# Attention and two MoE layers in one kernel: each engine's own register and branch in a weight change, low-part products last, attention's logits unjoined, and the order at the front and the border

## The chip, the cores and the metric

The kernel runs on one core of a Trainium2 chip. The metric is the device time of one execution in microseconds (us). A core has five engines with a queue of their own each, which run side by side and wait for one another through semaphores: PE (TensorE, the matmuls; its weight loads are listed as PEld), DVE (VectorE), ACT (ScalarE), POOL (GpSimd) and SP (SyncE, which here only starts transfers). An engine works through its queue strictly in order, so an instruction that waits holds up whatever stands behind it.

## The reference

The inputs are float32. Attention has 4 batches, 8 heads, 768 positions and 64 columns a head; a query sees 8 global and 96 local keys. Its output, as 3072 rows of 512, goes through a top-1 mixture of 8 experts with 1024 hidden units, and the result through a second one, whose logits also get a bias by modality.

```python
scores = scale * np.matmul(q, k.transpose(0, 1, 3, 2)) + bias   # masked: global or local keys
a = softmax(scores); attn = np.matmul(a, v)
x = attn.transpose(0, 2, 1, 3).reshape(3072, 512)
# MoE, twice with weights of its own
logits = x @ w_gate                  # second time: + modality_bias[modality_id]
expert_idx = np.argmax(logits, axis=1)
gate_w = softmax(logits)[arange(N), expert_idx]
for e in range(8):
    out[mask] = gate_w[mask, None] * (np.maximum(x[mask] @ w1[e], 0.0) @ w2[e])
```

## The kernel before

Every float32 operand of a product is split in a high part (float16) and a low part (bfloat16), and a product of two such operands is three matmuls: high by high, high by low, low by high.

**What sets the order.** `Timeline.at(t, fn)` gives each step a time that is a plain number, and `run` emits the steps sorted by it. The numbers come from the tables `OFF`, `MOFF`, `NEXTM`, `LASTM`, `LAST0` and `SOFF`. They don't make an instruction start at a time; they set in what order the steps stand in the queues of all engines, DMA issues included. The program is made under a manual schedule, so nothing reorders it later.

**Attention** works on 24 units of 128 queries, each with four head pairs. For a unit, PE computes the scores `sp` (L624, 24 products), DVE takes the row maximum `nm` (L636, one a head pair's half), ACT the exponentials `e`; PE transposes them (`et`, L653/654), ACT and DVE split them (`eh` L660, `el` L666), and PE multiplies by the values (`xp`, L681). DVE scales the sums to a row of the attention's output (`rs` L688, `row` L702). That row is then routed for the first MoE: PE transposes it (`xtp`, L712, step "rt"), ACT takes its high part (`rxh`, L717, step "rh"), DVE the low part (`rxl`, L722, step "rl"), PE forms the eight logits of each row (`lp`, L421, step "lg"), and DVE picks the largest: `join` (L428, L429) adds the two column groups of `lp` to `lg`, `MAX` (L437) and `MAX_INDEX` (L441) find the expert, L445 and L451 make a one-hot row `oh`. PE ranks it (`pr`, L472/473), DVE takes the position (`t`, L478), the count `acc` goes on (L482, on POOL in attention), and a scatter of POOL (L490) writes the row to a DRAM buffer `xs`, sorted by expert.

```python
ops = [(0, 2 * E, c) for c in range(4)] + [(1, E, c) for c in range(4)]      # logits, before: wg_hl holds
                                                                           # 8 high and 8 scaled low columns
```

**The MoEs** work on slots of 128 rows of one expert. A slot has four parts p of the hidden units. For each, `mm1` is 24 products (`hp`, L895), ACT and DVE split the result (`hh` L905, `hl` L906), and `mm2` is 6 products of 512 columns (`y`, L914). Weights in use lie in SBUF as h1, l1, h2, l2; if the next slot has another expert, `change` (L921, an `If` on a register read from a table) lets ACT cast the high part (`h`, L124) and DVE subtract the low part (`l`, L352) from float32 weights that were staged before. Such an `If` is in every engine's queue. `refill` (L934) is an `If` of SP, under which SP starts the transfers (`st`, L339) of an expert's weights, and "f00", "f01", "f10", "f11" are its four places in a slot. The first slots, FRONT (two in the first MoE, three in the second), are chosen before the whole table is known. After the fixed slots (27 and 23) a tail runs only if the count asks for it: `If` at L1107, also in every queue. Between the two MoEs the rows of the first are split (`r`, L955/956), stored (`x_d`, L970), loaded back transposed (`x2t`, L975), routed as above with a `join` of three operations (L428, L429, L431), and counted by the products `cp` (L497/498), from which DVE works out the second table. In the slots 17 to 19 of the first MoE SP also loads the rows of the second's three FRONT slots (step "lload": `mx` L847, `mm` L849, under the `If` at L1055).

The lines that the change touches moved in the changed kernel by 5 to 10; the prose uses those of the kernel before.

Of the kernel before, what the change touches and what calls it, by code (L numbers as in the profile page):

```python
# [12 lines left out]
BF16 = mybir.dt.bfloat16  # L13
# [54 lines left out]
NEXTM = {"p": 6.1, "pc": 6.2}  # L68
LAST0 = {
# [35 lines left out]
def kernel(  # L105
# [178 lines left out]
    wg_hl = [const.tile([128, 4, 2 * E], F16, name=f"wghl{m}") for m in range(2)]  # L284
    late = const.tile([32, 2], F32, name="late")
# [19 lines left out]
    def constants():  # L305
        nc.vector.tensor_scalar(out=rowoff_b, in0=rowoff[0:1, :], scalar1=-1.0, scalar2=None, op0=ALU.mult)
        nc.vector.memset(meta[:, :, 0:NM - E], 0.0)
        nc.vector.memset(meta[:, :, 2:3], 1.0)
        nc.vector.tensor_copy(out=meta[:, :, 1], in_=tok_id)
        nc.vector.tensor_copy(out=mod_f[:, 1], in_=mod_i[:, :, 0])  # L310
        nc.vector.tensor_scalar(out=mod_f[:, 0], in0=mod_f[:, 1], scalar1=-1.0, scalar2=1.0, op0=ALU.mult, op1=ALU.add)
        for i in range(2):
            nc.vector.tensor_tensor(out=mod_b[:, i], in0=mod_f[:, i].unsqueeze(2).to_broadcast([128, NU, E]),
                                    in1=bias_sb[:, i].unsqueeze(1).to_broadcast([128, NU, E]), op=ALU.mult)
        nc.vector.tensor_tensor(out=meta[:, :, NM - E:NM], in0=mod_b[:, 0], in1=mod_b[:, 1], op=ALU.add)
        for m in range(2):
            nc.vector.tensor_copy(out=wg_hl[m][:, :, 0:E], in_=wg_sb[m])
            nc.vector.tensor_tensor(out=wg_sb[m], in0=wg_sb[m], in1=wg_hl[m][:, :, 0:E], op=ALU.subtract)
            nc.vector.tensor_scalar(out=wg_hl[m][:, :, E:2 * E], in0=wg_sb[m], scalar1=LOW, scalar2=None, op0=ALU.mult)

        nc.vector.tensor_scalar(out=late[:, 0:1], in0=slot_id, scalar1=float(AHEAD), scalar2=None, op0=ALU.is_equal)
        nc.vector.tensor_scalar(out=late[:, 1:2], in0=slot_id, scalar1=float(AHEAD), scalar2=None, op0=ALU.is_gt)
# [94 lines left out]
    def logits(m, xt):  # L417
        lp = bank("C", "lp")
        ops = [(0, 2 * E, c) for c in range(4)] + [(1, E, c) for c in range(4)]
        for n, (x, w, c) in enumerate(ops):  # L420
            nc.tensor.matmul(out=lp[:, 0:w], lhsT=xt[x][:, c, :], rhs=wg_hl[m][:, c, 0:w],  # L421
                             start=(n == 0), stop=(n == len(ops) - 1), skip_group_check=True)
        return lp

    def join(lp, more=None):

        lg = small.tile([128, E], F32, tag="lg", name="lg")
        nc.vector.tensor_copy(out=lg, in_=lp[:, E:2 * E])  # L428
        nc.vector.scalar_tensor_tensor(out=lg, in0=lg, scalar=1.0 / LOW, in1=lp[:, 0:E], op0=ALU.mult, op1=ALU.add)  # L429
        if more is not None:  # L430
            nc.vector.tensor_tensor(out=lg, in0=lg, in1=more, op=ALU.add)  # L431
        return lg
# [453 lines left out]
    def mm1(m, s, p):  # L886
        d = mst[m][s]
        hp = bank("AD"[p % 2], "hp")[:, 0:256].rearrange("p (j c) -> p j c", j=2)
        for j in range(2):
            fs = slice(j * 128, (j + 1) * 128)  # L890
            n = 0
            for c in range(4):
                for w, x in ((h1, 0), (h1, 1), (l1, 0)):
                    r = d["x"][:, 4 * x + c, :]
                    nc.tensor.matmul(out=hp[:, j, :], lhsT=w[p][:, c, fs], rhs=r.bitcast(BF16) if x else r,  # L895
                                     start=(n == 0), stop=(n == 11))
                    n += 1
# [10 lines left out]
    def mm2(m, s, p):  # L908
# [3 lines left out]
        for j in range(2):  # L912
            for i, (hx, w) in enumerate((("hh", h2), ("hh", l2), ("hl", h2))):
                nc.tensor.matmul(out=d["y"], lhsT=d[hx, p][:, j, :], rhs=w[p][:, j, :],  # L914
                                 start=(p == 0 and j == 0 and i == 0), stop=(p == NP - 1 and j == 1 and i == 2))

    def change(m, s, p, i, step):

        if (m, s) not in regs:
            regs[m, s] = val(m, FCHG, s, [ET.Activation, ET.DVE], 1)  # L920
        with tc.If(regs[m, s] > 0):  # L921
            split(p, i, steps=(step,))
# [136 lines left out]
    def slots(tl, m, t0, t_table):  # L1059
# [21 lines left out]
        for s in range(fixed):  # L1081
# [9 lines left out]
            if m == 0:  # L1091
                offs = (LASTM if last else NEXTM if s == fixed - 2 else {}).items()
# [40 lines left out]
    for u in range(NU):  # L1133
# [3 lines left out]
        for nm, fn in (("tq", lambda u: t_in(u, "q")), ("tk", lambda u: t_in(u, "k")),  # L1137
# [3 lines left out]
                       ("lg", route_l), ("pm", lambda u: pick_m(st[u], join(st[u]["lp"]), st[u]["row"])),  # L1141
# [3 lines left out]
                       ("wa", lambda u: place_a(0, st[u], eng_of("wa"))), ("place", route_p)):  # L1145
# [73 lines left out]
```

## Time and profile before

| | us |
|---|---|
| three runs | 851.1, 852.2 (median), 865.14 |
| the profiled execution | 861.72 |
| its span | 860.2 |
| PE busy in the span | 775.3 (90%) |
| DVE busy | 485.0 (56%) |
| ACT busy | 395.5 (46%) |
| POOL busy | 311.0 (36%) |
| attention alone, with all engines full | 40 to about 200 |
| first MoE's fixed slots | about 228 to 560 |
| second MoE's fixed slots | about 604 to 846 |

Busy time is what an engine spent on instructions of its own, without branches, semaphores and DMA issues. The mean granted clock of TensorE was 0.976 of full speed. The profiled execution is some 9.5 us above the median of the three runs; sums are made against its 861.72.

### The profile page before, as it was taken

To read this page: it belongs to the slowest core of one execution; us is meant where nothing else is said; L and a number is where in the kernel's file an instruction comes from. 1 tells how busy PE (TensorE), PEld (TensorE's weight loads), DVE (VectorE), ACT (ScalarE), POOL (GpSimd) and SP (SyncE) were. 2 spreads that over 40 slices of the span, in tenths; PEclk is the share of its full clock that TensorE was granted. 3 is DMA by queue.
4 is the path that set the end of the run, shared out by engine and by line. 5 is a ranking of instruction groups with operands and counts; after the bars stand their busy time and mean duration, and the time that the engine had idled before them with its cause. 6 is when DMAs were issued, how large, how long until landed. Compare 5 with 4: busy or idle time off the path is not lost. (4 is left out here: it accounts for less than half of the span.)

```text
span 860.2 us, 29737 instructions
## 1 busy us (share of the span) xinstructions
PE 775.3 (90%) x9892; PEld 588.0 (68%) x9892; DVE 485.0 (56%) x1830; ACT 395.5 (46%) x859; POOL 311.0 (36%) x522
## 2 busy tenths in 40 slices
PE   4888988887799999999998898878999999999994
PEld 3777777776566777677766676555777777777773
DVE  4899999999627575757664747454111134111142
ACT  4788888788225253435523425331222244222251
POOL 5579887886532333233323241011111111111110
PEclk9899999998799999999999999999999999999998
DMA  8878676594666988898887877523822228222100
GB/s 138 226 194 235 152 181 157 135 299 127 236 141 181 217 197 248 255 192 238 230 222 174 221 199 185 155 57 72 242 66 53 52 78 219 61 54 56 41 26 18
DMA packets 227581, 133.97 MB, mean 156 GB/s; under 512 B 177148, under 2 KB 199676, under 8 KB 227360
## 3 DMA queue, kind: packets, MB, share of 16 engines
q1 hardware_dynamic: 220896, 112.10, 53.6%
q0 software_dynamic: 6320, 19.37, 6.1%
q8 instruction: 83, 1.36, 0.7%
q14 instruction: 138, 1.13, 0.5%
q10 hardware_dynamic: 144, 0.00, 0.0%
HBM read 79.54 MB, written 33.77 MB: 132 GB/s over the span
## 5 line engine op out<-in xcount | busy, mean ns | idle before, releaser
L895 PE MATMUL hp<-mx,h 128*128 128x128 f16 x3520 | 324.1, 221 | 7.7 <-ACTq L921 3.5
L895 PE MATMUL hp<-mx,l 128*128 128x128 f16 x1760 | 310.6, 221 | 13.7 <-DVE l L352 11.0
L895 PEld LDWEIGHTS <-h 128*128 128x128 f16 x3520 | 277.6, 99 | 46.0 <-issue 5.8
L906 DVE SCALAR_TENSOR_TENSOR hl<-hp,hh 128x256 bf16<-128x256 f32 x220 | 92.9, 423 | 255.2 <-ACT hh L905 131.3
L905 ACT ACTIVATE hh<-hp 128x256 f16<-128x256 f32 x220 | 84.0, 382 | 267.4 <-PE hp L895 234.6
L895 PEld LDWEIGHTS <-l 128*128 128x128 bf16 x1760 | 173.6, 99 | 15.6 <-DVE l L352 12.3
L914 PE MATMUL y<-h,hh 128*128 128x512 f16 x440 | 168.1, 382 | 0.0
L914 PE MATMUL y<-l,hh 128*128 128x512 bf16 x440 | 168.1, 382 | 0.0
L914 PE MATMUL y<-h,hl 128*128 128x512 f16 x440 | 167.6, 381 | 0.0
L352 DVE TENSOR_TENSOR l<-st,h 128x1024 bf16<-128x1024 f32 x84 | 105.4, 1256 | 42.5 <-ACTq L921 16.0
L914 PEld LDWEIGHTS <-hh 128*128 128x128 f16 x880 | 77.5, 98 | 53.8 <-issue 1.5
L124 ACT CAST h<-st 128x1024 f16<-128x1024 f32 x88 | 91.3, 1043 | 43.8 <-SPq L934 21.7
L964 POOL DMA_INDIRECT out_dram<-o,ti x26 | 27.2, 1045 | 227.7 <-ACTq L921 191.4
L490 POOL DMA_INDIRECT xs<-r,posi x29 | 33.4, 1153 | 181.1 <-DVEq L921 63.1
L643 ACT ACTIVATE e<-e,nm 128x232 f32<-128x232 f32 (+1 forms) x192 | 81.7, 471 | 6.2 <-DVE nm L636 5.7
L914 PEld LDWEIGHTS <-hl 128*128 128x128 bf16 x440 | 43.3, 98 | 53.1 <-issue 1.6
L666 DVE TENSOR_TENSOR el<-et,eh 128x512 bf16<-128x512 f32 (+1 forms) x96 | 60.9, 635 | 2.5 <-ACT eh L660 2.5
L636 DVE CUSTOM_DVE_ANT_0 e<-sp,bias_mid 128x232 f32<-128x232 f32 x160 | 58.0, 384 | 1.2 <-PE xp L681 0.8
L660 ACT CAST eh<-et 128x512 f16<-128x512 f32 (+1 forms) x96 | 51.9, 540 | 9.7 <-PE et L654 7.9
L624 PE MATMUL sp<-kt,qt 64*128 64x128 f16 (+3 forms) x1056 | 42.7, 219 | 14.3 <-DVE nm L636 14.1
L654 PE MATMUL et<-ident,e 128*128 128x128 f32 x192 | 48.4, 286 | 4.5 <-ACT e L643 2.2
L653 PE MATMUL et<-ident,e 128*128 128x128 f32 x160 | 43.0, 295 | 5.7 <-DVE el L666 2.8
(211 smaller groups left out, 1082.1 us busy)
## 6 DMA issues: line engine op xcount, KB each, us to landing
st<-in_moe_w_dram SPq DMA_DIRECT2D x88, 512.0 KB
mxf<-xs SPq DMA_DIRECT2D x29, 266.0 KB
x_d<-r SPq DMA_DIRECT2D x29, 256.0 KB
ld_k<-in_k_dram SPq DMA_DIRECT2D x24, 256.0 KB
ld_q<-in_q_dram SPq DMA_DIRECT2D x24, 256.0 KB
ld_v<-in_v_dram SPq DMA_DIRECT2D x24, 256.0 KB
row<-xg SPq DMA_DIRECT2D x24, 256.0 KB
xs<-empty SPq DMA_DIRECT2D x18, 266.0 KB
```

What stands on the lines that cost most here:

```text
L124: nc.scalar.copy(out=out, in_=in_)
L352: (nc.vector if engines[i][1] == "V" else nc.gpsimd).tensor_tensor(out=l, in0=w, in1=h, op=ALU.subtract)
L636: nc.vector.tensor_tensor_reduce(out=d["e", g][:, j, 0:w], in0=d["sp", g][:, j, 0:w], in1=(bias_mid if t else bias_first)[:, HEADS[g][j], ...
L643: nc.scalar.activation(out=e, in_=e, func=ACTF.Exp, bias=d["nm", g][:, j:j + 1], scale=-1.0)
L653: nc.tensor.transpose(tp[:, 2 + j, :], e[:, j, 0:128], ident)
L654: nc.tensor.transpose(tp[:, j, :], e[:, j, NA if t else 0:WB if t else 128], ident)
L660: nc.scalar.copy(out=eh[:, 0:n], in_=d["et", g][:, 0:n])
L666: nc.vector.tensor_tensor(out=el[:, 0:n], in0=d["et", g][:, 0:n], in1=d["eh", g][:, 0:n], op=ALU.subtract)
L895: nc.tensor.matmul(out=hp[:, j, :], lhsT=w[p][:, c, fs], rhs=r.bitcast(BF16) if x else r, start=(n == 0), stop=(n == 11))
L905: nc.scalar.activation(out=hh, in_=hp, func=ACTF.Relu)
L906: nc.vector.scalar_tensor_tensor(out=hl, in0=hp, scalar=0.0, in1=hh, op0=ALU.max, op1=ALU.subtract)
L914: nc.tensor.matmul(out=d["y"], lhsT=d[hx, p][:, j, :], rhs=w[p][:, j, :], start=(p == 0 and j == 0 and i == 0), stop=(p == NP - 1 and j == ...
```

## The change

1. **Attention's logits.** `logits(0, ...)` is now 12 products of 8 columns for each unit, all into the same 8 columns (high by high, high by a new constant `wg_l`, low by high), where there were 4 of 16 and 4 of 8. `join` is left out there: `MAX` and `MAX_INDEX` read `lp` in PSUM. In the MoEs `join` has two operations in place of three.
2. **`change`** gives the engine that splits a register and an `If` of its own (ACT's for the cast, DVE's for the subtraction), where one `If` for both stood in both queues for each step. Of 960 such compare-and-branch instructions on each of the two engines 480 are left.
3. **Products.** `mm1` does the 8 products of the high weights first and then the 4 of the low ones; `mm2` does the two by `l2` last.
4. **Tables.** The routing of a row (steps rt, rh, rl) stands earlier by 0.15 to 0.2 of a unit; the front slots and the lead loads ("lload") stand later; `PREVM` brings the last routing steps of slot `fixed - 4` to before the second border. The count of the last three units goes to DVE.

```diff
-    ... "rt": 10.15, "rh": 10.45, "lg": 11.9,
+    ... "rt": 10.0, "rh": 10.25, "lg": 11.9,
-    ... "rl": 10.75, ...
+    ... "rl": 10.6, ...
-    "front": 99.8, ... "lload": 2.4,
+    "front": 100.0, ... "lload": 3.6,
+PREVM = {"p": -0.15, "pc": -0.1}
...
+            if m == 0:
+                nc.vector.tensor_copy(out=wg_l, in_=wg_sb[m])
+                continue
...
     def logits(m, xt):
         lp = bank("C", "lp")
-        ops = [(0, 2 * E, c) for c in range(4)] + [(1, E, c) for c in range(4)]
-        for n, (x, w, c) in enumerate(ops):
-            nc.tensor.matmul(out=lp[:, 0:w], lhsT=xt[x][:, c, :], rhs=wg_hl[m][:, c, 0:w], ...)
+        if m == 0:
+            ops = [(x, w, E) for c in range(4) for x, w in ((xt[0][:, c, :], wg_hl[0][:, c, 0:E]),
+                                                           (xt[0][:, c, :], wg_l[:, c, :]),
+                                                           (xt[1][:, c, :], wg_hl[0][:, c, 0:E]))]
+        else:
+            ops = [(xt[i][:, c, :], wg_hl[1][:, c, 0:(2 - i) * E], (2 - i) * E) for i in range(2) for c in range(4)]
...
-    def join(lp, more=None):
+    def join(lp, more):
         lg = small.tile([128, E], F32, tag="lg", name="lg")
-        nc.vector.tensor_copy(out=lg, in_=lp[:, E:2 * E])
-        nc.vector.scalar_tensor_tensor(out=lg, in0=lg, scalar=1.0 / LOW, in1=lp[:, 0:E], op0=ALU.mult, op1=ALU.add)
-        if more is not None:
-            nc.vector.tensor_tensor(out=lg, in0=lg, in1=more, op=ALU.add)
+        nc.vector.scalar_tensor_tensor(out=lg, in0=lp[:, E:2 * E], scalar=1.0 / LOW, in1=more, ...)
+        nc.vector.tensor_tensor(out=lg, in0=lg, in1=lp[:, 0:E], op=ALU.add)
...
-            for c in range(4):
-                for w, x in ((h1, 0), (h1, 1), (l1, 0)):
+            ops = [(h1, x, c) for c in range(4) for x in range(2)] + [(l1, 0, c) for c in range(4)]
...
-        for j in range(2):
-            for i, (hx, w) in enumerate((("hh", h2), ("hh", l2), ("hl", h2))):
+        ops = [(hx, w, j) for hx, w in (("hh", h2), ("hl", h2), ("hh", l2)) for j in range(2)]
...
     def change(m, s, p, i, step):
-        if (m, s) not in regs:
-            regs[m, s] = val(m, FCHG, s, [ET.Activation, ET.DVE], 1)
-        with tc.If(regs[m, s] > 0):
-            split(p, i, steps=(step,))
+        eng = "V" if step else "A"
+        if (eng, m, s) not in regs:
+            regs[eng, m, s] = val(m, FCHG, s, [{"A": ET.Activation, "V": ET.DVE, "P": ET.Pool}[eng]], 1)
+        with tc.If(regs[eng, m, s] > 0):
+            split(p, i, (("A", eng), ("A", eng)), (step,))
...
-                offs = (LASTM if last else NEXTM if s == fixed - 2 else {}).items()
+                offs = (LASTM if last else NEXTM if s == fixed - 2 else PREVM if s == fixed - 4 else {}).items()
...
-    ("pm", lambda u: pick_m(st[u], join(st[u]["lp"]), st[u]["row"])),
+    ("pm", lambda u: pick_m(st[u], st[u]["lp"][:, 0:E], st[u]["row"])),
...
-    ("wa", lambda u: place_a(0, st[u], eng_of("wa"))), ...
+    ("wa", lambda u: place_a(0, st[u], eng_of("wa") if u < NU - 3 else nc.vector)), ...
```

**How instructions moved.** On DVE, in a middle unit of attention, before (`el` and `rs` belong to younger units, `lg` to the row that is routed):

```order
L702 TENSOR_TENSOR row<-xp,rs 128x256
L666 TENSOR_TENSOR el<-et,eh 128x512
L688 TENSOR_SCALAR rs<-xp 128x4
L428 COPY lg<-lp 128x8
L429 SCALAR_TENSOR_TENSOR lg<-lg,lp 128x8
L437 MAX row<-lg 128x8
L441 MAX_INDEX ix<-row,lg 128x8
L666 TENSOR_TENSOR el<-et,eh 128x512
```

The same place of DVE's queue in the changed kernel:

```order
L710 TENSOR_TENSOR row<-xp,rs 128x256
L674 TENSOR_TENSOR el<-et,eh 128x512
L696 TENSOR_SCALAR rs<-xp 128x4
L445 MAX row<-lp 128x8
L449 MAX_INDEX ix<-row,lp 128x8
L674 TENSOR_TENSOR el<-et,eh 128x512
```

Two rows went; the ones around them kept their places.

On PE, in attention, before, where the routed row is transposed; the 24 products `sp` of a unit's scores stand ahead of it, of which the last is shown:

```order
L624 LDWEIGHTS qt
L624 MATMUL sp<-kt,qt 128x128
L712 MATMUL xtp<-ident,row 128x128 x4
L654 MATMUL et<-ident,e 128x128 x2
L681 LDWEIGHTS eh
```

And in the changed kernel, from the last of the products `xp` on:

```order
L689 LDWEIGHTS el
L689 MATMUL xp<-vs_134,el 128x65
L720 MATMUL xtp<-ident,row 128x128 x4
L632 LDWEIGHTS qt
L632 MATMUL sp<-kt,qt 128x128
```

The four transposes of the row went from behind the 24 score products to ahead of them.

On SP, in slot 18 of the first MoE, before: a lead load (`mx`, `mm`, under the `If` at L1055), then the refill's `If` (L934) with its two transfers, then the transposed load `x2t`:

```order
L1055 COMPARE_AND_BRANCH
L847 ISA
L847 DMA_TRANSPOSE mx<-xs_84 128x8x128
L849 ISA
L849 DMA mm<-xs_84 128x20
L1055 UNCONDITIONAL_BRANCH x2
L921 UNCONDITIONAL_BRANCH x3
L830 TENSOR_LOAD slots_6593
L830 ISA x2
L934 COMPARE_AND_BRANCH
L339 ISA
L339 DMA st_0_163<-in_moe_w_dram 128x4x256
```

And in the changed kernel, from the same refill's `If` on:

```order
L941 COMPARE_AND_BRANCH
L344 ISA
L344 DMA st_0_164<-in_moe_w_dram 128x4x256
L344 ISA
L344 DMA st_1_165<-in_moe_w_dram 128x4x256
L941 UNCONDITIONAL_BRANCH x2
L982 DMA_TRANSPOSE x2t<-x_d 128x8x128
L928 UNCONDITIONAL_BRANCH
L1061 TENSOR_LOAD lead_i_193
L1061 ISA x2
L1062 COMPARE_AND_BRANCH
L855 ISA
```

The lead load went from ahead of the refill and of `x2t` to behind both.

## Rows read from the trace of the kernel before

**Rows 1.** Busy us (instructions) of PE, PEld, DVE, ACT, POOL by stretch; granted clock.

```profile
40.00:200.00 160.00, 138.44 (x2537) 120.03 (x2530) 153.25 (x732) 134.74 (x308) 133.25 (x215) 1.00 0.76 194
200.00:228.00 28.00, 17.03 (x229) 15.39 (x228) 21.28 (x83) 16.51 (x29) 20.35 (x23) 0.75 0.46 140
228.00:560.00 332.00, 313.88 (x3685) 228.11 (x3683) 197.26 (x618) 132.28 (x259) 99.99 (x173) 0.99 0.80 207
560.00:604.00 44.00, 35.81 (x414) 26.42 (x413) 22.68 (x111) 11.76 (x27) 6.56 (x9) 0.95 0.26 63
604.00:846.00 242.00, 242.00 (x2738) 176.17 (x2736) 63.25 (x177) 75.13 (x175) 28.94 (x45) 1.00 0.33 85
```

**Rows 2.** DVE's groups by line, 40 to 200 us: busy us, mean ns, idle before.

```profile
L722 DVE TENSOR_TENSOR rxl<-xtp,rxh 128x512 bf16<-128x512 f32 x20 | 13.7, 685 | 2.9 <-ACT rxh L717 2.9
...
L451 DVE TENSOR_SCALAR oh<-iota,ixf 128x8 bf16<-128x8 f32 x20 | 12.9, 643 | 0.0
...
L428 DVE COPY lg<-lp 128x8 f32<-128x8 f32 x21 | 3.2, 153 | 0.0
...
L445 DVE CAST ixf<-ix 128x1 f32<-128x1 uint32 x20 | 3.0, 148 | 0.0
```

**Rows 3.** What PE waited for, 230 to 440 us: in total, times, longest.

```profile
PE hp L895 <- DVE l L352: 5.0, 5, 1.7
```

**Rows 4.** What PE waited for, 440 to 560 us.

```profile
PE hp L895 <- DVE l L352: 5.7, 2, 3.1
PE hp L895 <- ACTq L921: 3.5, 2, 2.2
PE hp L895 <- DVEq L921: 2.7, 3, 1.0
```

**Rows 5.** Timeline of all engines before one wait: start, length, engine, what, idle before.

```profile
462.34 1.27 SPq L847 DMA_TRANSPOSE mx<-xs  x1
...
466.01 1.04 ACT L124 CAST h<-st 128x1024 f16<-128x1024 f32 x1 [3.88 <-SPq L934]
...
467.16 0.29 PE L895 MATMUL hp<-mx,h 128*128 128x128 f16 x2 [1.25 <-ACTq L921]
```

**Rows 6.** Timeline at the second border.

```profile
565.73 0.19 PE L472 MATMUL pr<-acc,ones_b 128*128 128x8 bf16 x1 [4.16 <-DVEq L1107]
```

**Rows 7.** Timeline of DVE within one unit of attention.

```profile
103.30 0.15 DVE L428 COPY lg<-lp 128x8 f32<-128x8 f32 x1
...
103.68 0.17 DVE L437 MAX8 row<-lg 128x8 f32<-128x8 f32 x1
...
106.03 0.42 DVE L702 TENSOR_TENSOR row<-xp,rs 128x256 f32<-128x256 f32 x1
...
107.03 1.04 DVE L451 TENSOR_SCALAR oh<-iota,ixf 128x8 bf16<-128x8 f32 x1
...
108.59 0.38 DVE L636 CUSTOM_DVE_ANT_0 e<-sp,bias_mid 128x232 f32<-128x232 f32 x1
```

**Rows 8.** Timeline of PE in the same unit.

```profile
106.17 0.78 PE L624 MATMUL sp<-kt,qt 64*128 64x128 f16 x23 [0.15 <-DVE nm L636]
...
106.88 0.65 PE L712 MATMUL xtp<-ident,row 128*128 128x128 f32 x4
...
109.64 0.18 PE L472 MATMUL pr<-acc,ones_b 128*128 128x8 bf16 x1 [0.83 <-DVE rxl L722]
```

**Rows 9.** Chain that ended last, 560 to 606 us: start, length, what.

```profile
573.25 1.40 PE hp L895 x22
...
575.98 1.36 PE hp L895 x24
```

**Rows 10.** What PE waited for, 206 to 228 us.

```profile
PE cp L497 <- POOL acc L482: 1.6, 1, 1.6
```

**Rows 11.** Instructions of line 921, the `If` of a weight change; durations in ns.

```profile
L921 DVEq COMPARE_BRANCH  x958: 43/56/74, 243.7 to 845.8; - x192
```

**Rows 12.** Instructions of line 1107, the `If` of the tail.

```profile
L1107 PEldq COMPARE_BRANCH  x1: 3793/3793/3793, 560.8 to 560.8; - x1
```

More of the change, by code (lines that the diff above doesn't have):

```diff
@@ L284 @@
     wg_hl = [const.tile([128, 4, 2 * E], F16, name=f"wghl{m}") for m in range(2)]
+    wg_l = const.tile([128, 4, E], BF16, name="wg_l")
     late = const.tile([32, 2], F32, name="late")
@@ L418, in logits @@
         lp = bank("C", "lp")
-        ops = [(0, 2 * E, c) for c in range(4)] + [(1, E, c) for c in range(4)]
-        for n, (x, w, c) in enumerate(ops):
-            nc.tensor.matmul(out=lp[:, 0:w], lhsT=xt[x][:, c, :], rhs=wg_hl[m][:, c, 0:w],
-                             start=(n == 0), stop=(n == len(ops) - 1), skip_group_check=True)
+        if m == 0:
[4 more added lines that the diff above has]
+            ops = [(xt[i][:, c, :], wg_hl[1][:, c, 0:(2 - i) * E], (2 - i) * E) for i in range(2) for c in range(4)]
+        for n, (x, w, k) in enumerate(ops):
+            nc.tensor.matmul(out=lp[:, 0:k], lhsT=x, rhs=w, start=(n == 0), stop=(n == len(ops) - 1),
+                             skip_group_check=True)
         return lp
-    def join(lp, more=None):
+    def join(lp, more):
         lg = small.tile([128, E], F32, tag="lg", name="lg")
-        nc.vector.tensor_copy(out=lg, in_=lp[:, E:2 * E])
-        nc.vector.scalar_tensor_tensor(out=lg, in0=lg, scalar=1.0 / LOW, in1=lp[:, 0:E], op0=ALU.mult, op1=ALU.add)
-        if more is not None:
-            nc.vector.tensor_tensor(out=lg, in0=lg, in1=more, op=ALU.add)
+        nc.vector.scalar_tensor_tensor(out=lg, in0=lp[:, E:2 * E], scalar=1.0 / LOW, in1=more, op0=ALU.mult, op1=ALU.add)
+        nc.vector.tensor_tensor(out=lg, in0=lg, in1=lp[:, 0:E], op=ALU.add)
         return lg
@@ L890, in mm1 @@
             fs = slice(j * 128, (j + 1) * 128)
-            n = 0
-            for c in range(4):
-                for w, x in ((h1, 0), (h1, 1), (l1, 0)):
[L894 to L897, printed above, removed]
+            ops = [(h1, x, c) for c in range(4) for x in range(2)] + [(l1, 0, c) for c in range(4)]
+            for n, (w, x, c) in enumerate(ops):
+                r = d["x"][:, 4 * x + c, :]
+                nc.tensor.matmul(out=hp[:, j, :], lhsT=w[p][:, c, fs], rhs=r.bitcast(BF16) if x else r,
+                                 start=(n == 0), stop=(n == 11))
         d["hp", p] = hp
@@ L911, in mm2 @@
             d["y"] = bank("B", "y")
-        for j in range(2):
-            for i, (hx, w) in enumerate((("hh", h2), ("hh", l2), ("hl", h2))):
-                nc.tensor.matmul(out=d["y"], lhsT=d[hx, p][:, j, :], rhs=w[p][:, j, :],
-                                 start=(p == 0 and j == 0 and i == 0), stop=(p == NP - 1 and j == 1 and i == 2))
+        ops = [(hx, w, j) for hx, w in (("hh", h2), ("hl", h2), ("hh", l2)) for j in range(2)]
+        for i, (hx, w, j) in enumerate(ops):
+            nc.tensor.matmul(out=d["y"], lhsT=d[hx, p][:, j, :], rhs=w[p][:, j, :],
+                             start=(p == 0 and i == 0), stop=(p == NP - 1 and i == len(ops) - 1))
     def change(m, s, p, i, step):
-        if (m, s) not in regs:
-            regs[m, s] = val(m, FCHG, s, [ET.Activation, ET.DVE], 1)
-        with tc.If(regs[m, s] > 0):
-            split(p, i, steps=(step,))
+        eng = "V" if step else "A"
[3 more added lines that the diff above has]
+            split(p, i, (("A", eng), ("A", eng)), (step,))
     def refill(m, s, k, i):
@@ L1140 @@
                        ("rt", route_t), ("rh", route_h), ("rl", route_lo),
-                       ("lg", route_l), ("pm", lambda u: pick_m(st[u], join(st[u]["lp"]), st[u]["row"])),
+                       ("lg", route_l), ("pm", lambda u: pick_m(st[u], st[u]["lp"][:, 0:E], st[u]["row"])),
                        ("pi", lambda u: pick_i(st[u], st[u]["row"])), ("pf", lambda u: pick_f(st[u], eng_of("pf"))),
@@ L1144 @@
                        ("wm", lambda u: place_m(0, st[u])), ("wt", lambda u: place_t(0, st[u])),
-                       ("wa", lambda u: place_a(0, st[u], eng_of("wa"))), ("place", route_p)):
+                       ("wa", lambda u: place_a(0, st[u], eng_of("wa") if u < NU - 3 else nc.vector)), ("place", route_p)):
             tl.at(SOFF.get(f"{nm}{u}", n + off_of(u, nm)), lambda u=u, fn=fn: fn(u))
```

8 rows, old and new, of tables (MOFF, OFF) are left out of this document.

## The prediction

> **What bounds the kernel now.** The first view is the busy time by stretch [rows 1], because each stretch has a limit of its own. From 40 to 200 us, attention, DVE works 153.25 of 160 us, so it sets the pace; PE has 160 - 138.44 = 21.6 us to spare there, ACT 25.3, POOL 26.8. From 228 to 560, the first MoE, PE works 313.88 of 332 and from 604 to 846 all of 242.00: there only PE's own products and the holes between them count. Between these lie the borders, with PE at 17.03 of 28 us and at 35.81 of 44. So a saved DVE operation is worth something in attention, a saved wait of PE in the first MoE and at the borders, and neither is worth anything from 604 on.
>
> Second come the views of where these engines wait. DVE's groups in attention [rows 2] show 2.9 us of idle time ahead of `rxl`, until ACT has made `rxh`; that is the largest part of the 6.75 us that DVE does not work. PE's waits in the first MoE are all for weights: 5.0 us in five waits for `l` up to 440 us [rows 3], then 5.7, 3.5 and 2.7 us [rows 4], 16.9 in all. The timeline tells of what kind one of them is [rows 5]: the cast waited 3.88 us for SP's refill branch (line 934), which stands behind a lead load that SP took from 462.34 on, and PE stood 1.25 us for the cast and then 1.0 more for the branch ahead of `l` (the longest of the three in [rows 4]). At the second border PE stands 4.16 us [rows 6].
>
> **The change, part by part.** *Logits unjoined.* DVE loses the two operations of L428 and L429. From the start of the first to the start of `MAX`, which comes next, is 103.68 - 103.30 = 0.38 us [rows 7]; that is what a unit loses. L428 ran 21 times in the stretch of 160 us [rows 2], so 20 to 21 of the 24 units lie where DVE sets the pace: 20.5 x 0.38 = 7.8 us, and I take 7.5, since some freed time will fall into a wait. The cover of the other engines is wide (21 us and more). Lower bound: if DVE's idle time of 6.75 us grows by 4.8, since what it waits for comes at a fixed distance behind, 3 us remain. Upper bound: all 24 units and no more waits for `rxh`, since its chain starts earlier, 9.1 + 2.9 = 12. The operations that stay now read PSUM; L428, which read PSUM, took 153 ns, L445, which reads SBUF, 148 [rows 2], so I set nothing against it. PE gets four more products a unit. The nearest rows are 23 `sp` products in the 0.71 us up to `xtp` [rows 8], 31 ns each, and 24 of `mm1` in 1.36 us [rows 9], 57 ns each; so 0.12 to 0.23 us a unit, some 4 us in all, in PE's spare 21.6: nothing.
>
> *Routing earlier (rt, rh, rl).* On PE `xtp` goes ahead of 24 score products. `xtp` runs for 0.65 us, and what follows it can start some 0.07 before its end, as `xtp` did behind `sp` (106.17 + 0.78 against 106.88, [rows 8]); so it takes 0.58. It needs `row`, which DVE ends at 106.03 + 0.42 = 106.45 [rows 7]. So PE will wait for `row` where it now makes scores, some 0.85 us, but loses the wait of 0.83 us for `rxl` ahead of `pr` [rows 8]. The scores then end at 106.45 + 0.58 + 0.78 = 107.8, or 108.1 with two hand-offs, each put at the 0.15 that PE waited for `nm` in front of `sp` [rows 8]; DVE takes its next row maximum at 108.59 [rows 7]. I cost it at nothing; the case in which that margin is gone is a rival. The wait for `rxh` may shrink; that is in the upper bound above.
>
> *First border and front.* PE stood 1.6 us ahead of `cp` until POOL had counted [rows 10]. For the last three units that is now DVE's, which took small operations in 0.15 us [rows 2], so some 1.4 us of it go. The pick is 0.38 us shorter. Taking both and a little of the rearranged front I take 2 us; 0 if the table that follows waits for the last scatter anyway, 4 if the front's `xtp` and `pr` ahead of 24 `hp` products open a part of the other 11 us that PE is idle there [rows 1].
>
> *Low-part products last, and a branch for each engine.* Within `mm1` the first use of `l` goes from the third product to the ninth: six products later, 6 x 57 ns = 0.34 us [rows 9]. The order costs nothing by itself, since the number of products and weight loads stays. In `change` DVE no longer passes ACT's branches, a compare of 56 ns [rows 11] and a jump of about as much each; three of them in the queue ahead of a late `l` make 0.3 us. The register load is one more for each engine and slot, and small beside it. So each of the five waits of [rows 3], 1.0 us on average, loses about 0.65: 3.3 us. The waits of the stretch after it [rows 4] are longer and come mostly from SP's transfers; 0.34 off a wait of 3.1 us would only be a bit of noise, so I count none.
> [...]
>
> *Lead loads behind the refill.* In slot 18 the refill's branch will be reached where the lead load stood, at about 462.3 rather than behind it, 3 us earlier; ACT casts from about 462.5 instead of 466.01 [rows 5], and PE's two waits go: 1.25 + 1.0 = 2.2 us. What is moved past is the transposed load `x2t` as well; the lead load comes some 3 us later, and it is needed only past 565 us. On SP two more instances follow in the slots next to it, with the same cover. Together with the term above 5.5 us; lower bound 1.6, the five waits less only 0.34 us each; upper bound 16.9, all waits for weights [rows 3, 4].
>
> *Second border.* The routing of slot `fixed - 4` no longer stands first behind the tail's `If`. PE waited there until 565.73, for DVE to pass that branch [rows 6]; its own branch at 560.8 took 3.79 us and ended at 564.6 [rows 12]. So PE could start 1.1 us earlier. But it meets a wait for `l` at 573.25 in the chain that ended last [rows 9], which then eats a part: `l` comes some 0.2 us earlier by the shorter join, and six more products, 0.34 us, go ahead of it. I take 0.6, 0 to 1.1. The table and the first fixed slot's load hang on the logits behind these products, so they move along.
>
> *Second MoE.* PE is full [rows 1]: nothing.
>
> The sum is 7.5 + 2 + 5.5 + 0.6 = 15.6 us: 861.7 becomes 846 in the profiled execution. The median of the three runs lies 9.5 us below it; none of the terms needs what makes that difference, so I take the sum off the median: 852.2 - 15.6 = 836.6.
>
> **The rivals.** *DVE's saving turns into waits.* Attention gives only the 3 us of its lower bound: 841. For it: ACT and POOL stand at 84% of the stretch, with bursts. Against: DVE waits only 6.75 us now.
> *The waits for weights are SP's.* The first MoE gives 1.6 instead of 5.5: 840.5. For it: the later half of the waits follows branches and transfers of SP [rows 4, 5], and PE that comes earlier only waits longer. Against: the first five end with DVE's `l`, not with a transfer [rows 3].
> *Both gains are full.* Attention 9, the MoE 12 of its 16.9, since a wait that ends earlier lets the weights of the next slot be freed and loaded earlier, the first border 3, the second 0.6: 24.6 off, 827.6.
> *The scores come late* (slower). If `xtp` ahead of the scores makes DVE wait for them, it waits in every unit. The margin above was 108.59 - 108.1 = 0.5 us, but in that unit the one-hot `oh`, which stands in between, took 1.04 us [rows 7], against a mean of 0.643 [rows 2], which leaves 0.1; and an `oh` as short as L445's 148 ns would leave -0.4. With hand-offs of 0.3 in place of 0.15 the loss is up to 0.7 us a unit, 20.5 x 0.7 = 14 us against the other 8.1: 858. It decides if, from the end of `row` to DVE's next row maximum, there is on average less than 0.58 + 0.78 + 0.3 = 1.7 us; in the unit shown there are 2.14. Against: the mean of `oh` still leaves 1.74.
> *Reading PSUM is dear.* `MAX` and the two passes of `MAX_INDEX` now read `lp` in PSUM. Between 5 ns more a pass (L428 against L445) and a whole operation's 150, about half of the 0.38 us would go: 840.5. Against: the 5 ns are measured, on small operations like these [rows 2].
> [...]
>
> **How the numbers follow.** My forecast has a chance of 0.45, the saving that turns into waits 0.14, SP's waits 0.13, both gains full 0.18, late scores 0.05, dear PSUM 0.05. The predicted time is the forecast's, 837. Its own range is 830 to 843. The range that leaves out 2 in 10 reaches from 825, which takes in most of the full gains, up to 850, which takes in two of the smaller gains at once (836.6 + 4.5 + 3.9 = 845) and some disturbance from the five tables that moved; only the late scores and the far ends stay outside. A measurement of this kernel can tell about 2% from no change, which here begins at 835.2. So faster by more than that holds the full gains (0.18) and something less than half of the forecast (0.21), 0.39 together; slower by more than 2% holds only the worse part of the late scores and what I have not thought of, 0.04; within 2% is the rest, 0.57.
>
> **What would show it.** In the changed profile, DVE's share from 40 to 200 us should stay near 95% and that stretch end some 7 to 8 us sooner; `MAX` should take about 170 ns as before; `xtp` on PE should wait for `row`, and DVE's row maximum should not wait for `sp`. `cp` should not wait for `acc`. The five waits for `l` up to 440 us should sum to under 2 us, and slot 18 should have no hole. PE's hole at the tail's `If` should be near 3 us. I am wrong if DVE shows new idle time ahead of the row maximum, if the waits for weights are as long as before with other releasers, or if transfers that start elsewhere collide with the refills.

## The result

The changed kernel takes 844.5 us (median of 12 runs), the kernel before 854.5 us in the 12 runs beside it: a ratio of 0.9893 with a 95% interval of 0.9869 to 0.9916, so 9 us faster (10 by the medians). The prediction took 15.6 us off 852.2, the median of the three runs known then, to 837, with a range of 825 to 850. The profiled execution has a span of 843.0 us and a granted clock of 0.972 on average.

The busy time of the changed kernel in the stretches of [rows 1]:

```profile
40.00:200.00 160.00, 141.01 (x2706) 124.73 (x2703) 152.07 (x722) 140.42 (x322) 135.06 (x220) 1.00 0.79 200
200.00:228.00 28.00, 18.05 (x206) 15.10 (x207) 23.45 (x92) 9.64 (x16) 17.42 (x17) 0.70 0.65 202
228.00:560.00 332.00, 314.37 (x3718) 229.23 (x3716) 191.33 (x559) 136.77 (x267) 108.38 (x173) 0.99 0.80 201
560.00:604.00 44.00, 41.79 (x493) 30.33 (x491) 18.17 (x103) 9.99 (x27) 6.83 (x10) 1.00 0.46 140
604.00:846.00 242.00, 227.93 (x2570) 165.38 (x2567) 60.82 (x166) 71.19 (x166) 28.41 (x44) 0.98 0.27 67
```

The stretches no longer cover the same work, since everything starts earlier, so the table below goes by events instead: the first `row` of unit 22 on DVE (units count from 0; end of attention), and the 5th, 116th and 133rd `hl` on DVE (into the first MoE, its end, into the second). The two columns of the kernel before are the profile that the prediction read, and a second one taken later.

| us | before, first | before, second | changed |
|---|---|---|---|
| attention, to the first event | 203.3 | 199.9 | 193.7 |
| first border | 38.1 | 38.1 | 39.7 |
| first MoE | 316.9 | 315.9 | 311.3 |
| second border | 58.1 | 55.6 | 54.6 |
| second MoE | 229.2 | 229.2 | 229.2 |

Against the second profile of before, attention gave 6.2 us, the first MoE 4.6, the second border 1.0, and the first border took 1.6. The profile that the prediction read was a long execution by some 7 us; that much was in attention (3.5) and at the second border (2.5).

DVE's groups in attention, 40 to 200 us, of the changed kernel (after the bar: busy us, mean ns, idle before), beside [rows 2]:

```profile
L644 DVE CUSTOM_DVE_ANT_0 e<-sp,bias_mid 128x232 f32<-128x232 f32 x144 | 52.1, 384 | 0.2 <-PE sp L632 0.2
...
L730 DVE TENSOR_TENSOR rxl<-xtp,rxh 128x512 bf16<-128x512 f32 x21 | 14.3, 682 | 3.3 <-ACT rxh L725 3.1
...
L459 DVE TENSOR_SCALAR oh<-iota,ixf 128x8 bf16<-128x8 f32 x21 | 9.4, 449 | 0.0
...
L449 DVE FIND_INDEX8 ix<-row,lp 128x8 uint32<-128x8 f32 x21 | 3.5, 165 | 0.0
...
L445 DVE MAX8 row<-lp 128x8 f32<-128x8 f32 x21 | 3.4, 161 | 0.0
...
L453 DVE CAST ixf<-ix 128x1 f32<-128x1 uint32 x21 | 3.1, 148 | 0.0
```

The pick of the kernel before, in the same stretch of its first profile:

```profile
L437 DVE MAX8 row<-lg 128x8 f32<-128x8 f32 x21 | 3.6, 170 | 0.7
...
L441 DVE FIND_INDEX8 ix<-row,lg 128x8 uint32<-128x8 f32 x21 | 3.4, 160 | 0.0
```

`MAX` takes 161 ns from PSUM, where it took 170 from SBUF, and the search 165 against 160: reading PSUM costs nothing that shows here. DVE waits 0.2 us for `sp` in the whole stretch. What PE waits for, 40 to 193 us:

```profile
PE xtp L720 <- DMA row<-xg: 13.7, 19, 1.9
```

That is `xtp` ahead of the scores, 0.7 us a unit where some 0.85 was forecast, in time that PE has. The line names a transfer into the same tile, but 15 of the 19 begin 0.14 to 0.16 us behind the end of DVE's `row`, which they were to wait for.

At the first border, what PE waits for from 206 to 228 us, beside [rows 10]:

```profile
PE xtp L720 <- DMA row<-xg: 2.4, 1, 2.4
...
PE lp L431 <- DVE t L486: 1.7, 1, 1.7
...
PE cp L505 <- DVE acc L490: 0.4, 1, 0.4
```

The wait for `cp` went from 1.6 to 0.4, and two came instead: 2.4 us ahead of the last unit's `xtp`, which did not wait in the kernel before and now begins 0.13 us behind DVE's `row`, and 1.7 for `t`. DVE's timeline shows what `t` waited for, the count that the change gave to DVE:

```profile
207.24 1.09 DVE L490 TENSOR_TENSOR acc<-acc,oh 128x8 bf16<-128x8 bf16 x1
...
211.62 4.13 DVE L490 TENSOR_TENSOR acc<-acc,oh 128x8 bf16<-128x8 bf16 x1 [1.32 <-PE pr L481]
```

and POOL's timeline what ran meanwhile:

```profile
206.19 2.12 POOL L357 TENSOR_TENSOR l<-st,h 128x1024 bf16<-128x1024 f32 x1
...
211.51 4.21 POOL L357 TENSOR_TENSOR l<-st,h 128x1024 bf16<-128x1024 f32 x2
```

An addition of 128x8 took 1.09 and 4.13 us. The first ends at 208.33, 0.02 us after POOL's split (206.19 + 2.12 = 208.31), the second at 215.75, 0.03 us after POOL's two splits that began at 211.51 (211.51 + 4.21 = 215.72).

In the first MoE, PE's waits from 228 to 430 us, beside [rows 3], and from 430 to 555, beside [rows 4] and [rows 6]:

```profile
PE hp L902 <- DVE l L357: 2.2, 2, 1.3
```

```profile
PE hp L902 <- DVEq L1114: 4.9, 1, 4.9
...
PE hp L902 <- DVE l L357: 2.8, 2, 2.5
...
PE hp L902 <- DVEq L928: 2.7, 2, 2.0
...
PE y L920 <- ACT hh L911: 2.0, 1, 2.0
...
PE hp L902 <- ACTq L928: 1.3, 1, 1.3
```

The five waits of 5.0 us in all became two of 2.2 in all. The lead loads did not do what they were to do. PE waits 2.03 us for `hh` at 454.50 and 2.03 for DVE's branch ahead of the products by `l` at 458.75, where the kernel before stood 2.2 us. The first of these goes back like this (POOL, ACT and PE of the changed kernel, idle time and what ended it in brackets):

```profile
450.09 1.03 POOL L498 DMA_INDIRECT xs<-r,posi  x1 [14.78 <-DMA mm<-xs]
...
453.49 0.30 ACT L471 ACTIVATE ex<-mm,nmx 128x8 f32<-128x8 f32 x1 [8.76 <-POOL nmx L466]
...
454.50 0.61 PE L920 MATMUL y<-h,hh 128*128 128x512 f16 x2 [2.03 <-ACT hh L911]
```

POOL stands 14.8 us ahead of a scatter of routed rows, until the lead load's `mm` has been read from `xs`; POOL's next steps, `nmx` (the bias of the softmax's exponential) among them, stand behind it; ACT's exponential stands for `nmx` 8.8 us, and `hh` behind that. The same place in the second profile of before:

```profile
454.62 1.04 POOL L490 DMA_INDIRECT xs<-r,posi  x1 [12.25 <-DVEq L921]
...
458.03 0.30 ACT L463 ACTIVATE ex<-mm,nmx 128x8 f32<-128x8 f32 x1 [4.25 <-POOL nmx L458]
```

There the scatter waits 12.3 us and ACT 4.3, and PE has no hole ahead of `hh`. The move of the load is not all of it: with all code edits and the old tables ACT waits 6.9 us at that place and PE 2.5 in two holes. But the hole ahead of `hh`, 1.1 to 2.9 us from the 61st `hl` to the 97th, is in all seven profiles that have the code edits and the new tables' lead loads, and in none of the seven others: neither with the tables alone nor with all code edits alone.

### The profile page after: what moved, and what is told of

Read it like the earlier page. It is cut to its first block, busy times and chain, and to the rows that moved or that the text cites. A ratio compares the mean times of both kernels' runs of the same rounds, so it can differ in the third digit from the quotient of the medians.

```text
span 843.0 us, 28986 instructions
## 1 busy us (share of the span) xinstructions
PE 768.9 (91%) x9988; PEld 585.8 (69%) x9988; DVE 472.7 (56%) x1756; ACT 393.4 (47%) x859; POOL 318.0 (38%) x519
## 5 line engine op out<-in xcount | busy, mean ns | idle before, releaser
L902 PE MATMUL hp<-mx,h 128*128 128x128 f16 x3520 | 272.0, 221 | 7.7 <-DVEq L1114 4.9
L902 PEld LDWEIGHTS <-h 128*128 128x128 f16 x3520 | 222.3, 99 | 46.4 <-ACTq L1114 5.3
L902 PE MATMUL hp<-mx,l 128*128 128x128 f16 x1760 | 172.1, 221 | 7.7 <-DVE l L357 5.0
L920 PE MATMUL y<-h,hh 128*128 128x512 f16 x440 | 130.9, 379 | 2.0 <-ACT hh L911 2.0
L920 PE MATMUL y<-l,hh 128*128 128x512 bf16 x440 | 130.9, 379 | 0.7 <-DVEq L928 0.7
L920 PE MATMUL y<-h,hl 128*128 128x512 f16 x440 | 130.9, 379 | 0.0
L357 DVE TENSOR_TENSOR l<-st,h 128x1024 bf16<-128x1024 f32 x84 | 107.1, 1277 | 36.3 <-ACTq L928 17.4
L902 PEld LDWEIGHTS <-l 128*128 128x128 bf16 x1760 | 118.1, 99 | 8.7 <-DVE l L357 5.7
L125 ACT CAST h<-st 128x1024 f16<-128x1024 f32 x88 | 91.2, 1043 | 43.9 <-SPq L941 10.2
L689 PEld LDWEIGHTS <-eh 104*128 104x128 f16 (+1 forms) x704 | 43.1, 99 | 3.7 <-ACT h L125 2.5
## 6 DMA issues: line engine op xcount, KB each, us to landing
mxf<-xs SPq DMA_DIRECT2D x29, 266.0 KB
xs<-empty SPq DMA_DIRECT2D x18, 266.0 KB
```

Of the source, the lines that this page charges most:

```text
L125: nc.scalar.copy(out=out, in_=in_)
L357: (nc.vector if engines[i][1] == "V" else nc.gpsimd).tensor_tensor(out=l, in0=w, in1=h, op=ALU.subtract)
```

## The experiments

Twelve kernels ran, in three groups of four on one chip each (the record numbers them 11, 0 and 0); the medians of the kernel before beside them are 854.8, 858.5 and 854.4 us. Ratios are to that kernel in the same group. Cuts in the code are marked by `...`.

**Logits alone, on the kernel before.**

```diff
-            ("pm", lambda u: pick_m(st[u], join(st[u]["lp"]), st[u]["row"])),
+            ("pm", lambda u: pick_m(st[u], st[u]["lp"][:, 0:E], st[u]["row"])),
```
with the 12 products of 8 columns and `wg_l` as in the change.

> The kernel before with attention's logits unjoined alone (12 products of 8 columns, MAX and MAX_INDEX from PSUM; the MoE joins, branches, product order and tables as before). My theory, that DVE sets attention's pace and loses 0.38 us a unit: 7 to 8 us faster (ratio 0.991), unit by unit in attention, with DVE still some 95% busy from 40 to 190 us, and nothing gained after it. Rival one, that the earlier routing is what the attention stage gained from: under 3 us here, with DVE's wait for rxh grown from 2.9 to 7 us or more. Rival two, that reads from PSUM are dear: MAX, MATCH_VALUE_LOAD and FIND_INDEX together over 0.5 us in place of 0.42, and about 4 us faster.

846.0 us, ratio 0.9889 (0.9857 to 0.9922); attention ends at 192.1 in place of 199.9. This edit alone gives as much as the whole change. DVE's one-hot row has changed with it, from a mean of 639 ns (first profile of before, 40 to 190 us; 539 in the second) to

```profile
L460 DVE TENSOR_SCALAR oh<-iota,ixf 128x8 bf16<-128x8 f32 x20 | 8.2, 409 | 0.0
```

so the 20.5 x 0.38 = 7.8 us are not all: 20.5 x 0.13 = 2.7 us came from `oh` and some 2.5 us went back into waits of DVE (4.1 us for `rxh` and 1.6 for `sp`, against 3.1 and none).

**Branches alone.**

```diff
+        eng = "V" if step else "A"
...
-            regs[m, s] = val(m, FCHG, s, [ET.Activation, ET.DVE], 1)
+            regs[eng, m, s] = val(m, FCHG, s, [{"A": ET.Activation, "V": ET.DVE, "P": ET.Pool}[eng]], 1)
...
```

> The kernel before with a register and a branch for each engine in a weight change, alone. My theory: each of the five waits for l up to 440 us loses about 0.3 us, so 1 to 2 us faster (ratio 0.998 to 0.999), all of it from 230 to 560 us. Rival, that the waits end with SP's and ACT's work: nothing, and the same five waits of 5.0 us in all.

854.4 us, 0.9992 (0.9967 to 1.0017). Not told apart from nothing, nor from the 1 to 2 us expected. In its profile PE's waits for `l` from 215 to 565 us sum to 5.8 us, against 10.7 and 8.9 in the two profiles of before, but those for ACT's branches to 6.0 against 3.5 and 1.0.

**Product order alone.**

```diff
+            ops = [(h1, x, c) for c in range(4) for x in range(2)] + [(l1, 0, c) for c in range(4)]
...
+        ops = [(hx, w, j) for hx, w in (("hh", h2), ("hl", h2), ("hh", l2)) for j in range(2)]
...
```

> The kernel before with the low-part products last in both matmul steps, alone. My theory: l is first used six products, 0.34 us, later, so five waits lose 1.7 us in all and the time is 1 to 3 us lower (ratio 0.997 to 0.999). Rival, that a wait that is shortened only moves to the next part, because DVE's splits come at a fixed rate: nothing, with the same sum of waits for l spread over more products. Other rival, that the later waits shrink too: 5 us.

854.1 us, 0.9991 (0.9963 to 1.0019): inconclusive in the same way. In its profile the waits for `l` from 215 to 565 us sum to 10.7 us, no less than in the two profiles of before (10.7 and 8.9).

**Tables alone.**

```diff
+    ... "rt": 10.0, "rh": 10.25, ... "rl": 10.6, ... "front": 100.0, ... "lload": 3.6, ...
+PREVM = {"p": -0.15, "pc": -0.1}
...
+    ... place_a(0, st[u], eng_of("wa") if u < NU - 3 else nc.vector) ...
```

> The kernel before with the tables of the changed one alone (routing steps earlier, front later, lead loads later, the last routing steps of slot fixed - 4 ahead of the border, the count of the last three units on DVE). My theory: nothing in attention, 2 us at the first border, 2.2 us from the lead loads, 0.6 at the second border: 3 to 5 us faster (ratio 0.995). Rival, that the earlier routing is what attention gains from: 8 us or more, with DVE's wait for rxh gone. Other rival, that transposes ahead of the scores make DVE wait for them: slower, with DVE idle time ahead of its row maximum.

856.5 us, 1.0012 (0.9992 to 1.0033): not faster. Attention ends at 199.2, so the earlier routing gains nothing there and loses nothing; the first border takes 39.8 us.

**All code edits, old tables.**

```diff
-    ... "rt": 10.0, "rh": 10.25, ... "rl": 10.6, ... "front": 100.0, ... "lload": 3.6, ...
+    ... "rt": 10.15, "rh": 10.45, ... "rl": 10.75, ... "front": 99.8, ... "lload": 2.4, ...
-PREVM = {"p": -0.15, "pc": -0.1}
...
-    ... place_a(0, st[u], eng_of("wa") if u < NU - 3 else nc.vector) ...
+    ... place_a(0, st[u], eng_of("wa")) ...
```

> All code edits of the change (logits, joins, branches, product order) with the tables of the kernel before. The prediction's sum gives the tables 4.8 us of the gain (first border 2, lead loads 2.2, second border 0.6): then about 849. Theory now, from the tables alone having gained nothing: the tables are worth nothing on top either, so 843 to 846, with the first border (last unit's row to the first MoE's fifth part) at 38.3 us instead of 39.7.

848.2 us, 0.9886 (0.9842 to 0.993): the same ratio as with the tables. The first border takes 37.8 us, the first MoE 309.6.

**Old routing steps, on the changed kernel.**

```diff
-    ... "rt": 10.0, "rh": 10.25, ... "rl": 10.6, ...
+    ... "rt": 10.15, "rh": 10.45, ... "rl": 10.75, ...
```

> The changed kernel with the old numbers of the routing steps (rt, rh, rl). Theory: transposes ahead of the scores make PE wait 13 us in all for the row, and with the shorter DVE chain that now shows; attention gets 1.5 us shorter, 842 to 844. Rival: DVE sets the pace in either order, so the same time within 0.5 us. Rival of the prediction, that the earlier routing shortens DVE's wait for rxh: up to 3 us slower than the changed kernel.

849.2 us, 0.9877 (0.9835 to 0.992): within the interval of the changed kernel. The first border is still 39.9.

**Old front, on the changed kernel.**

```diff
-    "front": 100.0, ...
+    "front": 99.8, ...
```

> The changed kernel with the old number for the front (99.8). Theory: the last unit's transposes and ranks then have 24 products of the first MoE in front of them as cover again, the waits of 2.4 us for the row and 1.7 us for the logits shrink, and the first border gets about 1.4 us shorter: 842 to 844. Rival, as predicted: the new order gains, and this is 1 to 2 us slower.

850.2 us, 0.9892 (0.9848 to 0.9935), first border 39.9: my theory, that the order of the front alone cost the 1.6 us, falls. The wait of 2.4 us ahead of the last `xtp` did go, but the one for `t`, which stands behind the count of 4.1 us on DVE, grew from 1.7 us by about as much:

```profile
PE lp L431 <- DVE t L486: 4.3, 1, 4.3
```

**Another operation for the one-hot row.** In [rows 7] `oh` runs from 107.03 to 108.07. POOL beside it, in the same profile:

```profile
106.88 1.16 POOL L583 TENSOR_TENSOR qt<-fq,qt 128x512 bf16<-128x512 f32 x1
```

ends at 108.04. Of the 20 `oh` of that profile from 40 to 200 us, 18 end like that, 0.02 to 0.04 us behind a POOL operation, after 0.23 to 1.25 us; the other two take 0.22.

```diff
-            eng.tensor_scalar(out=oh, in0=iota8, scalar1=d["ixf"], scalar2=None, op0=ALU.is_equal)
+            nc.vector.scalar_tensor_tensor(out=oh, in0=iota8, scalar=d["ixf"], in1=ones_b[:, 0:E],
+                                           op0=ALU.is_equal, op1=ALU.mult)
```

> The changed kernel with the one-hot row of attention made by another DVE operation, scalar_tensor_tensor with a constant of ones as the second operand, same result. Theory: the operation in use ends 0.02 us after the POOL operation that runs beside it, in every unit where it is long, so its mean of 0.45 us holds a wait for POOL; if the other operation does not wait, it takes 0.16 to 0.22 us each time, a unit loses 0.25 to 0.3 us, and the kernel 3 to 5 us: 840. Rival: it waits for POOL as well, or the time comes back as a wait for scores or rxh: no change.

848.5 us, 0.9869 (0.9829 to 0.9909), not told apart from the changed kernel; the rival was right in the time, and this operation is no shorter, 629 ns on average where the changed kernel's took 449:

```profile
L459 DVE SCALAR_TENSOR_TENSOR oh<-iota,ixf,ones_b 128x8 bf16<-128x8 f32 x20 | 12.6, 629 | 0.0
```

**The kernel before, again.** No edit.

> The kernel before, unchanged, for a second profile of it on the chip of the next three. If the first profile (861.72 us) held a slow execution, attention ends some 3 us earlier here and the whole takes 852 to 858 us; the second border lacks the 2.0 us wait and the slow clock behind it.

854.6 us, as expected; its stages stand in the table above.

**Count back on POOL, on the changed kernel.**

```diff
-    ... place_a(0, st[u], eng_of("wa") if u < NU - 3 else nc.vector) ...
+    ... place_a(0, st[u], eng_of("wa")) ...
```

> The changed kernel with the count of the last three units back on POOL. In the changed kernel DVE's count takes 1.09 and 4.13 us at the first border and ends with the POOL operation beside it. Theory: without it the border from the last unit's row to the first MoE's fifth part takes 38 in place of 39.7 us, 1.5 to 2 us faster than the changed kernel (ratio to before 0.987). Rival, as predicted: the count on DVE saves the 1.6 us that PE waits for POOL's count, so this is 1 to 2 us slower.

843.9 us, 0.9861 (0.982 to 0.9902), not told apart from the changed kernel; but in its profile the first border is 41.1 us, longer and not shorter, since PE waits for the count again:

```profile
PE cp L505 <- POOL acc L490: 2.7, 1, 2.7
```

So with the new front the count on DVE is worth 1.4 us of that border in these profiles, in spite of its 4.13 us, and the theory that it alone made the border longer falls.

**An accumulator on the one-hot row.**

```diff
-            eng.tensor_scalar(out=oh, in0=iota8, scalar1=d["ixf"], scalar2=None, op0=ALU.is_equal)
+            eng.tensor_scalar(out=oh, in0=iota8, scalar1=d["ixf"], scalar2=0.0, op0=ALU.is_equal, op1=ALU.add,
+                              accum_out=one)
```

> The changed kernel with attention's one-hot row made by the same operation as before but with an accumulator output that nobody reads. The operation on two SBUF inputs of the run before waited for POOL as well (mean 0.63 us). [...]

```profile
L460 DVE TENSOR_SCALAR_CACHE_REDUCE oh<-iota,ixf 128x8 bf16<-128x8 f32 x20 | 4.2, 211 | 0.0
L460 DVE DVE_READ_ACCUMULATOR oh<-iota,ixf 128x1 f32 x20 | 1.6, 82 | 0.0
```

From 40 to 190 us `oh` now takes 0.211 us on average, less than the shortest of the changed kernel (0.218), plus 0.08 to read the accumulator. Attention ends at 192.7, 3.3 us sooner than in the run above on the same chip, of the 20.5 x (0.51 - 0.29) = 4.5 us that `oh` saves, but 1.0 sooner than in the changed kernel. In all 845.3 us, 0.9879 (0.9838 to 0.9919): no gain of the whole kernel over the changed one is shown by this run, and that of attention rests on single profiles.

**Both.**

```diff
+            eng.tensor_scalar(out=oh, ..., accum_out=one)
...
+    ... place_a(0, st[u], eng_of("wa")) ...
```

> Both of these edits together on the changed kernel. Theory: 1.5 to 2 us at the border and 4 to 6 us in attention, so 6 to 8 us faster than the changed kernel (ratio to before 0.981 to 0.984). Rival: attention is then held by PE or ACT, and only the border's part stays (0.987).

840.6 us, 0.9825 (0.9782 to 0.9867), the lowest of all. Attention ends at 192.8, against 196.0 in the run that differs by the one-hot row alone; the 4 to 6 us that the theory has there were an estimate, for which these profiles show 3.2. The border of 41.3 us is no shorter, and PE's longest wait in it is

```profile
PE cp L507 <- POOL acc L492: 6.4, 1, 6.4
```

so the theory's part on the border is wrong although the time came out as it said. Its median is 4.7 us below that of the run above on the same chip, which differs by the count alone, and 3.3 below that of the count back on POOL, which differs by the one-hot row alone, both with overlapping intervals; what the count on POOL would give back later, if anything, is not found. The interval lies just below that of the changed kernel (0.9869 to 0.9916, from another group of runs).

## Why the prediction was right, and where its sum was not

The time fell into the range, and the forecast's largest term is shown; but 9 to 10 us came of the 15.6, and the 852.2 that the sum was taken off was 2.3 below the median of twelve runs.

**Attention (7.5 us).** Right, and shown: the logits alone give 0.9889. Its working missed a part. DVE's busy time holds waits for POOL, inside `oh`, as its ends say (18 of 20 lie 0.02 to 0.04 us behind a POOL operation in the first profile of before), and with the 0.38 us that went `oh` changed too, from a mean of 639 and 539 ns to 409 with the logits alone; that DVE shifted against POOL is my reading of it. Six profiles with unjoined logits and the old `oh` end attention between 192.1 and 201.1 us; in the one at 201.1 `oh` takes 706 ns on average, and it ran in the group whose kernel before is slowest, 858.5 us. How much of that spread is `oh` and how much the group is open, since the kernel before was not profiled there.

**Scores late, dear PSUM, gain eaten.** The first two did not come: 0.2 us of waits for `sp`, and 418 ns for the three passes from PSUM (161 + 92 + 165) against 422; the half of the 0.38 us that dear PSUM was to take is shown by no run. The third came in part: with the logits alone some 2.5 us went back into waits, and it is by luck that the shorter `oh`, which the sum did not count, gave as much.

**First border (2 us off).** This is the step that failed: it is 1.6 us longer. The price of the count on DVE, "which took small operations in 0.15 us", came from operations that took 147 to 158 ns each time from 40 to 200 us (L428, L445); the count took 1.09 and 4.13 us. The gain ahead of `cp` was real (1.6 to 0.4). The new front, counted as a small gain, put the 24 products `hp` behind the last unit's `xtp` that had stood ahead of it and covered its wait for `row`. What PE waits for at this border, in all fourteen profiles:

| front | last count on | profiles | for the last `row` | for `t` | for the count | border |
|---|---|---|---|---|---|---|
| old | POOL | 6 | none | none | 1.4 to 1.7 | 37.8 to 38.5 |
| old | DVE | 1 | none | 4.3 | 0.4 | 39.9 |
| new | POOL | 2 | 2.2 and 2.3 | none | 6.4 and 2.7 | 41.3 and 41.1 |
| new | DVE | 5 | 2.1 to 2.4 | 1.7 to 1.8 | 0.4 | 39.7 to 40.4 |

So the front and the count each opened a wait, and whoever puts one of them back meets more of the other's. The old routing steps change none of these waits: the profile that has them with the new front and the count on DVE lies with the others of its row. Old front and POOL's count together, with the new routing steps, were not run; the six profiles of the first row have the old steps too, so that the two alone would bring back the 38 us is argued from the waits.

**First MoE (5.5 us off).** The size was about right: 316 us in the two profiles of before, 309.7 to 314.4 in seven with all the code edits and the new lead loads, on average 312.0, so 4 us. The part for the five waits was about right (5.0 to 2.2 us where 3.3 off were forecast; less 0.34 each, the lower bound is 1.7 and not 1.6). Of its 0.65 us a wait, the jump put beside each compare is shown by no run; three of these branches in a row began within 0.3 us on DVE in the first profile of before (266.0 to 266.3), as much as the sum has for them. The register load is not one more: DVE has 51 of them in either profile, with a median of 0.30 and 0.31 us. PE's waits were not all for weights, as the prediction read them: in the stretch of [rows 3] stands

```profile
PE hp L895 <- DMA mx<-mxs: 1.2, 1, 1.2
```

as well, which is gone in the changed kernel. The part for the lead loads was wrong: "it is needed only past 565 us" overlooked who waits for the load to finish reading, POOL's scatter into the same buffer, and through it ACT and PE; the hole was to go, and there are 4.1 us of holes. The move by itself was not run, so its share of them is argued from the chain of waits, not shown; but the stage's gain needs nothing of it, since with all code edits and the old tables it takes 309.6 us. The later waits, at which I counted nothing, made up for it, and that the size came out near the forecast is luck in so far: from the 97th `hl` to the 116th it took 57.3 us in the second profile of before and 53.7 in the changed one. Branches and product order by themselves show nothing that can be measured (0.9992, 0.9991).

**Second border (0.6 us off).** About right in size (1.0), by another way, and not shown to come from the table: with the logits alone and with all code edits and the old tables this border takes 54.9 us, against 54.6. PE's hole was to be near 3 us and is 4.9: PE still starts behind DVE's passing of the tail's branch, although its first work is now `mm1`.

Between the second profile of before and that of the changed kernel that makes 6.2 + 4.6 + 1.0 - 1.6 = 10.2 us, and 9 by the ratio, where 7.5 + 5.5 + 0.6 + 2 = 15.6 were forecast; the first border alone is 3.6 of the difference. By the medians, the logits explain all of it (0.9889 against 0.9893), and the rest of the change adds nothing that these intervals can tell.

## What to carry to other kernels

Where an engine sets the pace, count what its busy time is made of: a small operation whose length varies by a factor of five (`oh`, 0.22 to 1.25 us) may be waiting inside itself. Two edits at one place can each open a wait that the other covers in part, so that undoing one of them shows nothing: look at the waits, and undo them together too. A transfer moved later in one queue is not done when its issue is cheap: look for who writes the buffer that it reads, and what stands behind that writer. Take a second profile of the kernel before where terms of 2 us are summed: the first one here held 7 us that were not the kernel's.

## What the runs showed of the hardware

**Some of DVE's instructions end with one of POOL's.** `tensor_scalar` from SBUF (`oh`) took 0.22 to 1.25 us in the first profile of before, and 18 of 20 ended 0.02 to 0.04 us behind a POOL operation. The count with two SBUF inputs took 0.16, 1.09 and 4.13 us in the changed kernel; the two long ones ended 0.02 and 0.03 us behind POOL's splits. `scalar_tensor_tensor` with two SBUF inputs, in the place of `oh`, took 0.63 us on average. With an accumulator output `tensor_scalar` took 0.211 us on average there, and 0.08 for the read. The profile counts the long time as busy time of the DVE instruction (1.04 us for one `oh` in [rows 7]). What holds these instructions, and why the form with the accumulator stays short, is not shown.

**Behind a hole of 2 us the clock fell in one profile and stayed in another.** At the second border of the first profile of before, PE stood 2.04 us for `mx`. The granted clock was 1.00 from 595 to 602 us; behind the hole it fell to 0.72 on average over 602 to 608 us (columns as in [rows 1], PEclk is the third number from the right), and to 0.50 from 603 to 606:

```profile
602.00:608.00 6.00, 5.79 (x55) 4.20 (x56) 0.42 (x1) 0.78 (x3) 0.18 (x1) 0.72 0.94 220
```

and the 24 products behind the hole took 2.02 us instead of 1.36 [rows 9], by the chain that ended last:

```profile
602.21 2.02 PE hp L895 x24
```

In the profile of the product order alone PE stood 2.02 us for `mx` at the same place, and the clock behind it stayed at 1.00; the 24 products took 1.50 us:

```profile
596.20:602.00 5.80, 5.79 (x70) 4.39 (x71) 1.19 (x5) 1.48 (x5) 0.18 (x1) 1.00 0.89 216
```

```profile
596.21 0.61 PE L894 MATMUL hp<-mx,h 128*128 128x128 f16 x8 [2.02 <-DMA mx<-xs]
```

```profile
596.21 1.50 PE hp L894 x24
```

In the changed kernel the hole there is 0.48 us, and the clock stays too:

```profile
586.70:592.00 5.30, 5.24 (x60) 3.88 (x61) 0.91 (x3) 1.16 (x4) 0.18 (x1) 1.00 0.59 149
```

So the length of that hole alone does not say whether the clock falls behind it; what else decides is not found here.
